# The experts' raw weight chunks in eight rooms, the second unit's list completed on TensorE, the late rows stored from ScalarE's queue

## The chip, the cores and the metric

The kernel runs on one core of one Trainium2 chip. The time is that of one execution on the device, in microseconds; a kernel's time is the median of several executions. Beside it stands one profiled execution, whose trace gives every instruction and DMA; times in the trace count from the start of its span.

## What is computed

The reference is a chain of three layers on 1792 tokens of 768 features:

```
scores = scale * q @ k.T, causal;  x = softmax(scores) @ v        # 4 x 12 heads, 448 x 64
h = x @ w_in;  g = h - tanh(h);  x = g @ w_out                    # 768 -> 2048 -> 768
e_idx = argmax(x @ w_gate)                                        # 8 experts, one for each token
gate_w = softmax(x @ w_gate)[e_idx];  eom = sigmoid(x @ w_output_gate)
out[mask] = gate_w * eom[e] * (relu(x[mask] @ w1[e]) @ w2[e])     # 768 -> 1024 -> 768
```

All data is float32, and which expert a token goes to is known only when its row of the second layer's output is.

## The kernel before

**Precision.** In the large matmuls a float32 operand is split in two parts, a rounded high part (ScalarE, `copy` to float32r) and the rest (VectorE, raw minus high), and three products are summed in PSUM: high by high, high by rest, rest by high. So each weight chunk of 128 x 768 costs a ScalarE cast (line 79) and a subtraction (line 80) before TensorE can use it. The split chunks lie in a ring of slots (class `Weights`, lines 51 to 86), which is filled round and round; a slot is free when the last matmul on its chunk is done.

**Stages.** Attention and the first dense matmul (`attention_mlp1`) run to about 444 us. Then `mlp2_route` makes the second dense layer tile by tile: 14 tiles of 128 tokens, each in two halves of 384 features (`mlp2`, matmuls on line 604), 48 matmuls a half. A tile's rows are stored to the scratch tensor `x2s` in DRAM (line 872, SP's queue). The routing of earlier tiles runs beside it: for the first eleven tiles VectorE multiplies the rows with the eight gate rows, which lie spread over all partitions in `rowsE` (24 KB a partition, lines 564 to 567; the products on line 627); for the last three tiles, and so for the *late* ones, 12 and 13, TensorE turns the rows (`turn`, line 642) and makes the logits (`logits`, line 655). `choose` takes the best expert of each token, `place` counts its position in the expert's list, and `send` (line 761) scatters token number and weight into the list tensor `lst` in DRAM from GpSimd's queue, one scatter for each tile, the second after the first has landed.

**The experts' units.** `experts` works in nine units of up to 256 tokens with one expert's weights, 16 chunks each: eight chunks of w1 (`up`, line 957, 18 matmuls of 256 columns for each chunk) and eight of w2 (`down`, line 977, four calls of 24 matmuls of 384 columns: two token halves `t` by two feature halves `o`). A unit's rows are gathered from `x2s` by an indirect DMA on GpSimd (`gather`, line 908) and turned and split (`split`, lines 945 to 948: twelve transposes in three groups, two PSUM buffers). The results are scattered to the output (`put`, line 989).

The first unit starts early: when tiles 0 to 11 are routed, `begin_with` (lines 775 to 798) picks the fullest expert so far, and its first 256 tokens become the first unit, which needs none of the late tiles. The late tiles' tokens of that expert are placed behind its 256th position (`skip`). The other eight units are the experts 0 to 7 in order, and all their lists are read together, after the late tiles have been sent: `get_lists` (line 825, from GpSimd's queue), then `pick_lists` (line 829: two transposes on line 899, products, `allids` and `allcf` on lines 840 and 841).

**The order of the work.** The Tile framework keeps an order for each engine near that of the program and lets an instruction pass others that are not ready in its own model. Steps of the routing hang in a list `steps` with a due time, counted in quarters of a half-tile (`boundary`, line 845). What is still due when the second layer ends is handed to `experts` as `late`: two steps after each `up` of the first unit (line 1020), the last one, `pick_lists`, in `leave` after the first `down` (line 1027). `leave` also closes the routing's PSUM pool and opens another in its place, so that a `down` behind it can't begin before `pick_lists` has read its PSUM tile; then it gathers the second unit's rows.

**The weights' way.** Raw chunks pass through four stage buffers. The 16 chunks of the first unit are all loaded in the last half of the second layer, one after each of its 16 steps (line 612, `fetch`), each `load` being an SP DMA into a stage buffer, a cast on ScalarE and a subtraction, five of them on GpSimd (`LO_GPSIMD`) and the others on VectorE. Then each `up` is followed by one load and each `down` by two (lines 1018 and 1031). `leave` adds six slots to the ring's 16.

```
 612             after()
1019                 W.append(load(jobs.pop(0)))
1026                 down(hs, W2, y, cu[:, c0 + t:c0 + t + 1], t, o)
1027                 if u == 0 and (t, o) == (0, 0):
1028                     leave()
1029                 if (t, o) == ((1, 0) if u == 0 else (0, 0)) and nxt:
1030                     x = split(xg)
```

## Time and profile before

| | us |
|---|---|
| median of three executions (lowest, highest) | 1043.81 (1043.26, 1045.07) |
| profiled execution, its own time | 1041.34 |
| span of its trace | 1039.7 |
| TensorE busy in it | 995.6 |
| VectorE, ScalarE, GpSimd busy | 656.9, 496.2, 82.0 |

The profiled execution took 1.6 us more than its span, and 2.5 us less than the median of the three others. "PE" is TensorE's matmuls and "PEld" its weight loads, DVE is VectorE, ACT ScalarE, POOL GpSimd, SP SyncE. Durations of matmuls overlap, so that a row of many matmuls is read by its start and by the start of the next row.

### The profile page before, as it was taken

The numbers are of one execution on the slowest core, as the hardware profiler recorded it, in microseconds if no ns is written. First come the engines' busy times: TensorE is split into PE (matmuls) and PEld (weight loads), VectorE is DVE, ScalarE is ACT, GpSimd is POOL, SyncE is SP. The second block draws the span as 40 slices with busy tenths as digits, with TensorE's granted clock in tenths as the row PEclk, the third lists the DMA queues.
The fourth block names the chain that finished last, engine by engine and source line by source line (L and its number), as shares of the span: only waits on it lengthen the run. The fifth ranks groups of instructions, "written<-read, shape, count | busy, mean of one in ns | idle before, by whom it ended". The sixth has DMA issues, their size and how long they took to land.

```text
span 1039.7 us, 16458 instructions
## 1 busy us (share of the span) xinstructions
PE 995.6 (96%) x6068; PEld 891.3 (86%) x6068; DVE 656.9 (63%) x1461; ACT 496.2 (48%) x1027; POOL 82.0 (8%) x87
## 2 busy tenths in 40 slices
PE   8998999999999999999999999986999999999995
PEld 3555788888878888999999999976899999999994
DVE  5888898878787635435767686265556555754520
ACT  5878786677666534311212121253545544654420
POOL 1000000000000000000111112132210111010000
PEclk9999999999999999999999999998999999999998
DMA  8534567566675328452424334376967756764500
GB/s 300 157 131 133 159 176 226 180 213 209 188 212 182 114 92 255 147 217 72 128 88 140 108 91 137 115 240 158 311 190 249 225 191 214 252 205 154 186 14 32
DMA packets 88203, 176.48 MB, mean 170 GB/s; under 512 B 8694, under 2 KB 51944, under 8 KB 87858
## 3 DMA queue, kind: packets, MB, share of 16 engines
q1 hardware_dynamic: 83682, 158.15, 49.0%
q0 software_dynamic: 4272, 16.96, 5.0%
q8 instruction: 49, 0.80, 0.3%
q14 instruction: 40, 0.33, 0.1%
q10 hardware_dynamic: 160, 0.23, 0.1%
HBM read 142.80 MB, written 34.08 MB: 170 GB/s over the span
## 4 chain that ended last, share of the span: by engine, by line
PE 70%; DMA 11%; DVE 8%; ACT 5%; issue 4%; POOL 1%; SPq 1%; POOLq 0%; ACTq 0%; DVEq 0%
PE x2p L604 21%; PE h L414 14%; PE py L977 12%; PE h L957 10%; DMA wraw<-in_w_dram 5%; PE x L391 3%; DMA wo<-dy 3%; PE pt L371 3%; PE s L306 2%; PE s L315 2%; ACT w L79 2%; DMA glo<-gT 1%; DVE w L80 1%; PE warm L436 1%; DVE pr L332 1%
## 5 line engine op out<-in xcount | busy, mean ns | idle before, releaser
L604 PE MATMUL x2p<-w,ghi 128*128 128x384 f32 x896 | 228.7, 336 | 0.0
L414 PE MATMUL h<-xh,w 128*128 128x448 f32 x768 | 225.7, 372 | 1.6 <-DVE g L421 1.0
L80 DVE TENSOR_TENSOR w<-wraw,w 128x768 fp32r<-128x768 f32 x139 | 131.4, 961 | 62.9 <-ACT w L79 61.7
L977 PE MATMUL py<-w,h 128*128 128x384 f32 x864 | 158.2, 340 | 3.9 <-ACT h L963 3.1
L79 ACT CAST w<-wraw 128x768 fp32r<-128x768 f32 x144 | 117.4, 833 | 92.9 <-DMA wraw<-in_w_dram 56.4
L957 PE MATMUL h<-xh,w 128*128 128x256 f32 x864 | 157.9, 285 | 3.9 <-DVE h L964 2.1
L604 PEld LDWEIGHTS x2p<-w,ghi 128*128 128x128 f32 x896 | 161.1, 188 | 0.2 <-issue 0.2
L977 PEld LDWEIGHTS py<-w,h 128*128 128x128 f32 x864 | 150.4, 190 | 4.8 <-ACT h L963 3.4
L604 PE MATMUL x2p<-w,glo 128*128 128x384 f32 x448 | 149.8, 334 | 0.0
L414 PEld LDWEIGHTS h<-xh,w 128*128 128x128 f32 x768 | 138.5, 188 | 11.9 <-DVE g L421 2.2
L414 PE MATMUL h<-xl,w 128*128 128x448 f32 x384 | 141.4, 369 | 0.0
L957 PEld LDWEIGHTS h<-xh,w 128*128 128x128 f32 x864 | 135.2, 192 | 6.3 <-DVE h L964 3.4
L957 PE MATMUL h<-xl,w 128*128 128x256 f32 x432 | 123.1, 285 | 0.1
L341 ACT ACTIVATE pr<-pr,mx 128x128 f32<-128x128 f32 (+3 forms) x168 | 88.8, 529 | 54.8 <-DVE mx L332 53.8
L627 DVE CUSTOM_DVE_ANT_0 junk<-x,rowsE 128x768 bf16<-128x768 f32 x88 | 84.2, 957 | 33.8 <-ACT x L613 31.5
L604 PEld LDWEIGHTS x2p<-w,glo 128*128 128x128 f32 x448 | 84.1, 188 | 0.2 <-issue 0.2
L957 PEld LDWEIGHTS h<-xl,w 128*128 128x128 f32 x432 | 83.2, 193 | 0.3 <-DVE xl L948 0.3
L332 DVE CUSTOM_DVE_ANT_0 pr<-s,mask 128x384 f32<-128x384 f32 (+2 forms) x144 | 59.9, 420 | 29.1 <-PE s L306 21.4
L414 PEld LDWEIGHTS h<-xl,w 128*128 128x128 f32 x384 | 72.0, 188 | 4.3 <-DVE xl L403 0.2
L371 PE MATMUL pt<-ident,pr 128*128 128x128 f32 x384 | 61.8, 276 | 1.3 <-ACT pT L378 0.4
L421 DVE TENSOR_TENSOR g<-h,g 128x448 f32<-128x448 f32 x64 | 39.8, 621 | 34.1 <-ACT g L420 34.0
L391 PE MATMUL x<-pT,v 128*64 128x448 f32 (+3 forms) x384 | 58.0, 399 | 0.3 <-ACT pT L378 0.3
(156 smaller groups left out, 1160.0 us busy)
## 6 DMA issues: line engine op xcount, KB each, us to landing
wraw<-in_w_dram SPq DMA_DIRECT2D x144, 384.0 KB, 3.9
gT<-g SPq DMA_DIRECT2D x64, 224.0 KB, 2.5
glo<-gT SPq DMA_DIRECT2D x14, 1024.0 KB, 5.9
draw<-in_w_out_dram SPq DMA_DIRECT2D x16, 768.0 KB, 4.8
raw<-in_w_in_dram SPq DMA_DIRECT2D x14, 768.0 KB, 5.3
q<-in_qk_dram SPq DMA_DIRECT2D x36, 240.0 KB, 4.1
k<-in_qk_dram SPq DMA_DIRECT2D x36, 224.0 KB, 3.7
wo<-dy SPq DMA_DIRECT2D x16, 384.0 KB, 5.3
```

The source lines that it names most:

```text
L79: self.nc.scalar.copy(t[:, 0, :], raw)
L80: lo_engine.tensor_tensor(t[:, 1, :], raw, t[:, 0, :].bitcast(F32), op=ALU.subtract)
L332: nc.vector.tensor_tensor_reduce(out=self.probs(r), in0=ss[:, o:o + w], in1=m, scale=-0.125, scalar=3.0e38, op0=ALU.add, op1=ALU.min, accu ...
L341: nc.scalar.activation(pc, pc, AF.Exp, bias=self.mx[:, x:x + 1], scale=-1.0, accum_out=self.sm[:, x:x + 1],)
L371: nc.tensor.transpose(pt[:, n * P:(n + 1) * P], self.pr[:, o:o + P], ident)
L391: nc.tensor.matmul(px[j * D:(j + 1) * D, kc * P:], self.v[:n, kc, j, :], self.pT[:n, j, pcol[kc]:pcol[kc] + S - kc * P], start=(kc == 0), ...
L414: nc.tensor.matmul(ph, w[:, kd, :], x, start=(n == 0), stop=(n == 3 * KD - 1))
L421: nc.vector.tensor_tensor(g, ph, g, op=ALU.subtract)
L604: nc.tensor.matmul(px, a[:, f, :], w[:, 0, h * hn:(h + 1) * hn], start=(n == 0), stop=(n == 3 * NF - 1),)
L627: nc.vector.tensor_tensor_reduce(out=junk, in0=x2, in1=row, scale=1.0, scalar=0.0, op0=ALU.mult, op1=ALU.add, accum_out=to,)
L957: nc.tensor.matmul(ph, wp[:, kd, :], a[:, kd].rearrange("p a b -> p (a b)"), start=(n == 0), stop=(n == 3 * KD - 1),)
L977: nc.tensor.matmul(py, hs[f][a][:, c], w[:, 0, o * hn:(o + 1) * hn], start=(n == 0), stop=(n == 3 * KF - 1),)
```

## The change

- `Supply` holds eight *rooms* of 128 x 768. At first they hold the eight gate rows (one DMA each in place of two for four rows each); when `begin_with` is through, the first unit's and all experts' chunks are entered, and `fill` issues DMAs into rooms as they come free. `load` splits the next raw chunk and calls `fill`. Only the first eight chunks are split in the last half of the second layer (after its steps 0 to 7), the other eight after the first unit's `up`s. All subtractions are VectorE's. The ring grows by two slots and not by six, and two more chunks are loaded after the first unit.
- The second unit is now expert 0 from a list of its own, `early`: `get_early` reads that expert's list as the first twelve tiles left it, `pick_early` turns it, and `add_late` adds the late tiles' tokens with one-hot matmuls on TensorE; then it gathers the rows. The list of the other seven is read as before, but `leave` comes after the third `down` of the first unit.
- The late steps go one, one, two, two, one after the first five `up`s (`LATER`), `turn` before them.
- The rows of tiles 12 and 13 are stored from ScalarE's queue and not from SP's.

```diff
+LATER = (1, 1, 2, 2, 1, 0, 0, 0)
-LO_GPSIMD = (3, 4, 7, 13, 15)
...
-    def split(self, raw, a, lo_engine):
+    def split(self, raw, a):
         t = self.slot()
         self.nc.scalar.copy(t[:, 0, :], raw)
-        lo_engine.tensor_tensor(t[:, 1, :], raw, t[:, 0, :].bitcast(F32), op=ALU.subtract)
+        self.nc.vector.tensor_tensor(t[:, 1, :], raw, t[:, 0, :].bitcast(F32), op=ALU.subtract)
-    def load(self, stage, src, a, lo_engine):
-        raw = stage.tile([P, 768], F32, tag="wraw", name="wraw")
-        self.nc.sync.dma_start(raw, src)
-        return self.split(raw, a, lo_engine)
...
+class Supply:
+    def __init__(self, nc, ring, pool, nrooms):
+        self.nc, self.ring, self.pool, self.n = nc, ring, pool, nrooms
+        self.pos = 0
+        self.todo, self.raws, self.W = [], [], []
+    def room(self, i, name):
+        return self.pool.tile([P, 768], F32, tag=f"room{i}", name=name, bufs=1)
+    def add(self, chunks):
+        self.todo.extend(chunks)
+    def fill(self):
+        while self.todo and len(self.raws) < self.n:
+            src, a = self.todo.pop(0)
+            raw = self.room(self.pos, "wraw")
+            self.nc.sync.dma_start(raw, src)
+            self.raws.append((raw, a))
+            self.pos = (self.pos + 1) % self.n
+    def load(self):
+        if self.raws:
+            self.W.append(self.ring.split(*self.raws.pop(0)))
+            self.fill()
+    def take(self, n):
+        W = self.W[:n]
+        del self.W[:n]
+        return W
...
-    rowsE = dotp.tile([P, E, DM], F32, name="rowsE")
-    for h in range(2):
-        s = slice(h * E // 2, (h + 1) * E // 2)
-        nc.sync.dma_start(rowsE[:, s], gates[s].unsqueeze(0).to_broadcast([P, E // 2, DM]))
+    rowsE = [supply.room(e, f"row{e}") for e in range(E)]
+    for e in range(E):
+        nc.sync.dma_start(rowsE[e], gates[e:e + 1].to_broadcast([P, DM]))
...
+        one = w12[bass.ds(first[0], 1)].rearrange("e f p c -> (e f) p c")
+        supply.add(weight_chunks(one, KD, w12.shape[1] // 2))
+        for e in range(E):
+            supply.add(weight_chunks(w12[e], KD, w12.shape[1] // 2))
+        supply.fill()
...
+    def get_early():
+        src = lst.rearrange("(r b) c -> r (b c)", b=P)[0:4, :]
+        early.append(fetch_list(nc, sp, src, 4))
+    def pick_early():
+        pt = turn_list(nc, ps, early[0], 4, ident)
+        both = sp.tile([P, 2, 2, 2], F32, tag="both0", name="both0", bufs=1)
+        for r in range(2):
+            nc.vector.tensor_scalar_mul(
+                both[:, r], pt[:, :, 2 * r:2 * r + 2], is1[:, r, 0:1]
+            )
+        had = sp.tile([P, 2, 2], F32, tag="had", name="had", bufs=1)
+        nc.vector.tensor_tensor(had, both[:, 0], both[:, 1], op=ALU.add)
+        start = sp.tile([P, 1], F32, tag="start", name="start", bufs=1)
+        nc.vector.tensor_scalar(
+            start, is1[:, 1, 0:1], -2.0 * P, 1.0, op0=ALU.mult, op1=ALU.add
+        )
+        early.extend([had, start])
+    def add_late(route):
+        _, had, start = early
+        N = route.n
+        v = sp.tile([P, 2], F32, tag="v", name="v", bufs=1)
+        nc.vector.scalar_tensor_tensor(
+            v, route.po, start, route.oh[:, :, 0], op0=ALU.add, op1=ALU.mult
+        )
+        to = sp.tile([P, 2, 2 * P], F32, tag="to", name="to", bufs=1)
+        add = sp.tile([P, 2, 2], F32, tag="add", name="add", bufs=1)
+        nc.vector.tensor_scalar_add(add[:, :, 0], tok[:, LATE:LATE + N], -float(NT))
+        nc.vector.tensor_copy(add[:, :, 1], route.pr[:, :, 1])
+        for m in range(N):
+            nc.vector.tensor_scalar(
+                to[:, m], slots, v[:, m:m + 1], None, op0=ALU.is_equal
+            )
+        pq = ps.tile([P, 2, 2], F32, tag="tr", name="late")
+        for t in range(2):
+            for m in range(N):
+                nc.tensor.matmul(
+                    pq[:, t, :], to[:, m, t * P:(t + 1) * P], add[:, m, :],
+                    start=(m == 0), stop=(m == N - 1),
+                )
+        for n, nm in enumerate(("ids", "cf")):
+            nc.vector.tensor_tensor(
+                consts["early" + nm], pq[:, :, n], had[:, n, :], op=ALU.add
+            )
+        early.append(gather(nc, consts["xg"], x2s, consts["earlyids"], 0))
...
-                mlp2(t, g, x2, h, (lambda: fetch(first[0])) if last else None)
+                mlp2(t, g, x2, h, (lambda f: f < NF // 2 and supply.load()) if last else None)
...
-            nc.sync.dma_start(x2s[t * P:(t + 1) * P, :], x2)
+            put = nc.scalar if t >= LATE else nc.sync
+            put.dma_start(x2s[t * P:(t + 1) * P, :], x2)
...
         if t0 + N == LATE:
-            then += [(6, begin_with), (11, begin_x)]
+            then += [(6, begin_with), (7, get_early), (11, begin_x), (12, pick_early)]
         if t0 + N == NTT:
+            then[-1:-1] = [(p, lambda r=route: add_late(r))]
             then += [(9, totals), (9, get_lists), (13, pick_lists)]
...
-    jobs = [job for e in range(E) for job in weight_chunks(w12[e], KD, KF)]
-    todo = [(consts["ids"], consts["cf"], 0)]
-    todo += [(consts["allids"], consts["allcf"], 2 * e) for e in range(E)]
+    todo = [(consts[nm + "ids"], consts[nm + "cf"], 0) for nm in ("", "early")]
+    todo += [(consts["allids"], consts["allcf"], 2 * e) for e in range(1, E)]
     x = split(xg)
+    late.pop(0)()
     def leave():
-        nonlocal ps, xg
+        nonlocal ps
         while late:
             late.pop(0)()
         route_close()
         rp = ctx.enter_context(tc.tile_pool(name="ring2", bufs=1))
-        ring.add_slots(rp, 6)
+        ring.add_slots(rp, 2)
         ps = ctx.enter_context(tc.tile_pool(name="exps", bufs=2, space=PSUM))
-        xg = gather(nc, consts["xg"], x2s, todo[1][0], todo[1][2])
     for u, (iu, cu, c0) in enumerate(todo):
-        W1, W2, W = W[:KF], W[KF:2 * KF], W[2 * KF:]
         nxt = todo[u + 1] if u + 1 < len(todo) else None
         if u > 0 and nxt:
             xg = gather(nc, consts["xg"], x2s, nxt[0], nxt[2])
         hs = []
+        W1 = supply.take(KF)
         for f in range(KF):
             hs.append(up(x, W1[f], f))
-            if jobs:
-                W.append(load(jobs.pop(0)))
-            for _ in range(2):
-                if len(late) > 1:
+            supply.load()
+            if u == 0:
+                for _ in range(LATER[f]):
                     late.pop(0)()
+        if u == 0:
+            xg = early[-1]
+        W2 = supply.take(KF)
         for t in range(2):
             y = sp.tile([P, DM], F32, tag="y", name="y")
             for o in range(2):
                 down(hs, W2, y, cu[:, c0 + t:c0 + t + 1], t, o)
-                if u == 0 and (t, o) == (0, 0):
-                    leave()
                 if (t, o) == ((1, 0) if u == 0 else (0, 0)) and nxt:
                     x = split(xg)
                 for _ in range(2):
-                    if jobs:
-                        W.append(load(jobs.pop(0)))
+                    supply.load()
+                if u == 0 and (t, o) == (1, 0):
+                    leave()
             put(y, iu[:, c0 + t:c0 + t + 1])
+        if u == 0:
+            for _ in range(2):
+                supply.load()
...
-        consts["stage"] = ctx.enter_context(tc.tile_pool(name="stage2", bufs=4, side="right"))
+        rooms = ctx.enter_context(tc.tile_pool(name="rooms", bufs=1, side="right"))
+        consts["supply"] = Supply(nc, ring, rooms, E)
```

## Rows read from the trace of the kernel before

**Rows 1.** The page's second part: TensorE's busy tenths in 40 slices of the span.

```profile
PE   8998999999999999999999999986999999999995
```

**Rows 2.** Busy time by stage: stretch, us, then each engine, granted clock, DMA share, GB/s.

```profile
682.46:741.98 59.52, 45.29 (x293) 41.30 (x292) 34.68 (x70) 27.98 (x49) 18.18 (x14) 0.89 0.75 217
741.98:780.03 38.05, 36.19 (x254) 35.31 (x253) 22.95 (x32) 19.71 (x32) 4.05 (x4) 1.00 0.71 226
780.03:815.99 35.96, 35.68 (x254) 35.21 (x253) 20.71 (x30) 18.09 (x29) 3.95 (x4) 1.00 0.67 216
816.15:851.37 35.22, 35.22 (x255) 34.95 (x254) 20.76 (x30) 17.99 (x29) 3.95 (x4) 1.00 0.67 215
725.00:730.00 5.00, 4.43 (x18) 4.46 (x19) 3.98 (x10) 3.03 (x4) 3.56 (x3) 0.66 0.44 117
```

**Rows 3.** The chain that ended last, fourth unit: start us, us, what.

```profile
816.15 17.11 PE h L957 x144
833.27 4.17 PE py L977 x24
837.43 0.87 PE tr L945 x8
```

**Rows 4.** TensorE in order of time around the first unit; idle time before in brackets.

```profile
682.46 1.03 PE L945 MATMUL tr<-ident,xg 128*128 128x128 f32 x8
...
685.63 0.98 PE L957 MATMUL h<-xh,w 128*128 128x256 f32 x6 [1.58 <-ACT xh L947]
...
693.42 0.63 PE L655 MATMUL lg<-x2T,gw 128*32 128x256 f32 x6 [2.21 <-ACT x2T L645]
...
695.67 0.87 PE L671 MATMUL g<-fold,lgT 128*128 128x16 f32 x4
...
717.86 0.80 PE L977 MATMUL py<-w,h 128*128 128x384 f32 x2 [3.05 <-ACT h L963]
...
724.52 0.44 PE L899 MATMUL ltr<-ident,li 32*128 32x32 f32 x2 [4.93 <-DMA li<-lst]
725.57 9.87 PE L977 MATMUL py<-w,h 128*128 128x384 f32 x48 [0.60 <-DVE allids L840]
```

**Rows 5.** GpSimd's timeline in the same stretch.

```profile
659.31 0.96 POOL L761 DMA_INDIRECT lst<-pr,sl  x1 [9.82 <-DVE sl L754]
663.86 0.59 POOL L892 DMA_DIRECT2D li<-lst  x1 [3.59 <-DMA lst<-pr,sl]
672.14 1.05 POOL L908 DMA_INDIRECT xg<-x2s,ids  x1 [7.69 <-DVE cf L804]
...
704.92 1.54 POOL L761 DMA_INDIRECT lst<-pr,sl  x1 [1.60 <-DVE ov L822]
713.62 0.98 POOL L761 DMA_INDIRECT lst<-pr,sl  x1 [7.16 <-DMA lst<-pr,sl]
719.47 0.64 POOL L892 DMA_DIRECT2D li<-lst  x1 [4.87 <-DMA lst<-pr,sl]
```

**Rows 6.** ScalarE's timeline: a DMA issue at the start, and the first unit.

```profile
1.54 0.87 ACTq L264 DMA_DIRECT2D k<-in_qk_dram  x1
...
683.21 0.47 ACT L613 COPY x<-x2p 128x384 f32<-128x384 f32 x1
...
713.60 0.83 ACT L79 CAST w<-wraw 128x768 fp32r<-128x768 f32 x1 [3.53 <-DMA wraw<-in_w_dram]
```

**Rows 7.** Instructions on the experts' raw chunks: ns min/median/max, first and last start.

```profile
L80 DVE TENSOR_TENSOR w<-wraw,w x139: 936/959/1732, 675.4 to 991.1; 128x768 fp32r<-128x768 f32 x139
...
L80 POOL TENSOR_TENSOR w<-wraw,w x5: 1837/1935/2475, 677.6 to 701.4; 128x768 fp32r<-128x768 f32 x5
```

**Rows 8.** DMA issues between 662 and 668 us, KB each, us to landing.

```profile
x2s<-x SPq DMA_DIRECT2D x1, 384.0 KB, 4.4
```

**Rows 9.** DMA landings on the tensor of the second layer's rows.

```profile
DMA to landing us min/median/max: 2.7/5.1/10.5
```

**Rows 10.** DMA landings of the gathers, line 908.

```profile
DMA to landing us min/median/max: 3.8/4.6/10.5
```

More of the change, by code (lines that the diff above doesn't have):

```diff
@@ L535, in split_w @@
     def split_w(f):
-        wout.append(ring.split(raws.pop(0), 1, nc.vector))
+        wout.append(ring.split(raws.pop(0), 1))
         fetch_w(f + 4)
@@ L590, in mlp2_route @@
     )
+    slots = cp.tile([P, 2 * P], F32, name="slots")
+    nc.gpsimd.iota(
+        slots, pattern=[[1, 2 * P]], base=1, channel_multiplier=0,
+        allow_small_or_imprecise_dtypes=True,
+    )
     ones = cp.tile([P, P], BF16, name="ones")
@@ L841, in pick_lists @@
         nc.vector.tensor_tensor(consts["allcf"], both[:, 0, 1], both[:, 1, 1], op=ALU.add)
-    steps, first = [], []
+    steps, first, early = [], [], []
     def boundary(now):
@@ L886, in mlp2_route @@
     consts["rtps"] = ps
-    return first[2], [st for _, st in sorted(steps, key=lambda x: x[0])], ctx.close
+    late = [st for _, st in sorted(steps, key=lambda x: x[0])]
+    return first[2], early, late, ctx.close
 def fetch_list(nc, pool, src, n):
@@ L919, in weight_chunks, with experts @@
         yield e[f], KD if f < KF else 1
-def experts(tc, consts, ring, load, W, xg, late, route_close, w12, x2s, lst, out):
+def experts(tc, consts, ring, xg, early, late, route_close, w12, x2s, lst, out):
     nc = tc.nc
@@ L1081, in fused @@
     consts = dict(ident=ident, S=S, D=D, NP=NP, B=NT // S)
-    for nm, n in (("", 2), ("all", 2 * E)):
+    for nm, n in (("", 2), ("early", 2), ("all", 2 * E)):
         consts[nm + "ids"] = cp.tile([P, n], I32, name=nm + "ids")
@@ L1105, in fused @@
     last = attention_mlp1(tc, consts, ring, qk, v, w_in, w_out, wo, gT)
-    def load(job):
-        n = consts["nload"] = consts.get("nload", -1) + 1
-        return ring.load(consts["stage"], *job, nc.gpsimd if n in LO_GPSIMD else nc.vector)
-    W, first = [], []
-    def fetch(e):
-        if not first:
-            one = w12[bass.ds(e, 1)].rearrange("e f p c -> (e f) p c")
-            first.extend(weight_chunks(one, DM // P, KF))
-        W.append(load(first[len(W)]))
-    xg, late, close = mlp2_route(tc, consts, ring, last, wo, gw, gates, gT, x2s, lst, fetch)
-    experts(tc, consts, ring, load, W, xg, late, close, w12, x2s, lst, out)
+    xg, early, late, close = mlp2_route(
+        tc, consts, ring, last, wo, gw, gates, w12, gT, x2s, lst
+    )
+    experts(tc, consts, ring, xg, early, late, close, w12, x2s, lst, out)
 def laid_out(np, q, k, v, moe_w_in, moe_w_out, moe2_w_gate, moe2_w_output_gate, moe2_w1, moe2_w2):
```

25 lines of the change are left out of this document (16 added, 9 removed).

## The prediction

> **What bounds the kernel now.** The slices come first [rows 1]: TensorE is at 9 tenths nearly throughout, with one dip behind slice 26, some 680 to 760 us. Nothing outside it is worth much to this change, which touches neither attention nor the first dense layer. The stages size the dip [rows 2]: the first unit, from the end of the second layer to the first `up` of the next, takes 59.52 us, the second 38.05, the third 35.96, the fourth 35.22 with TensorE busy all the time. The fourth's pace is the matmuls themselves [rows 3]: 144 `up`s in 17.11, four `down`s of 4.17, twelve transposes in some 1.4. Three units at that pace would be 105.7; they take 133.5. So about 28 us are lost, and not all can come back: the first unit also holds its own transposes and the routing of the late tiles.
>
> TensorE's order of time says who holds it [rows 4]. The first `up` begins 3.2 us after the first transpose. Later come 2.21 us for `x2T` on ScalarE, 3.05 for a relu on ScalarE, and 4.93 for the list of all experts, with 1.05 more from its transposes to the next `down`. Behind the first two of these stands a late weight: ScalarE's casts wait for their DMAs, as at 713.60 [rows 6], and relus and copies queue behind them. After the long wait the granted clock is 0.66 of full, between its levels of 1.2 and 2.4 GHz [rows 2], and 48 matmuls take 9.87 us [rows 4] where two `down`s take 8.3 [rows 3]: 1.5 us on top. The list's 4.93 has a chain of its own on GpSimd [rows 5]: first scatter at 704.92, second only when it has landed, at 713.62, the list's read at 719.47, landed at 724.5.
>
> **The change part by part.** *Rooms.* Eight raw chunks are asked for at about 662 us, 12 us before the last half of the second layer, and afterwards eight are always on their way in place of four. At 4.4 us to land [rows 8] the first eight are there before their casts begin; the waits for weights go. Casts and subtractions remain. The five subtractions of GpSimd, 1.9 us each, become five of VectorE, 0.96 each [rows 7]: 4.8 us, costed at nothing, because VectorE was busy 34.7 of the first unit's 59.5 us [rows 2], and even all of that with these 4.8 and an estimated 1.5 for the late list's small operations is 41 of the 43 us that I expect of the unit. It is near: where subtractions bunch, VectorE is what is late next, at 0.96 a chunk. The gate rows' eight DMAs in place of two move the same bytes, hidden by the first tile's half-layers; costed at nothing.
>
> *Late rows from ScalarE.* An issue on ScalarE takes 0.87 us in the nearest row [rows 6], against the wait and the cast that now stand between its copy at 683.21 and the first `up` at 685.63. Two issues, one of them on the path: I let them cancel most of the gain and take 685.0 as the first `up` (bounds 684 and 686.5). SP is then free for the loads; the store shares the DMA engines with them.
>
> *The second unit's list.* `add_late` adds four float32 matmuls of two columns. The nearest row has two matmuls of 16 columns, four records, in 0.87 us at a lowered clock [rows 4]; so 1.7 at most, nothing if they fall into waits, and I take 0.9. The two small transposes of `pick_early` and the VectorE operations lie beside the second layer. On GpSimd two gathers, 1.05 us of issue each [rows 5], now stand before the scatters of the late tiles, and `out`'s scatters behind all of it.
>
> *The first unit, summed.* First `up` 685.0; `up`s 17.1; routing left on TensorE 2.0 (an estimate from the 0.63 and 0.87 of [rows 4] and the turn) and the new 0.9; three `down`s 12.5; transposes for the second unit 1.4. These can't hide under the fourth `down`, which stands behind `leave`: between 0 and the 3.2 us that the same chain left uncovered at 682.46; I take 1.1, since no store stands in it. That is 720.0. Then the list's transposes and `allids`, 1.05 as before: 721.05.
>
> *The list's wait* is what is late next. The scatter comes after four `up`s in the program, 696 at the earliest; before it came at 704.92, which with two gathers makes 707.0 at the latest; I take 701, as the chain from `x2T` to `sl` loses 2.2 us of waiting and its VectorE operations the company of GpSimd's. From first scatter to landed list before took 19.6 [rows 4, 5]; with both scatters at the 4.55 from 659.31 to 663.86 and the read's 5.0 it is 14.1. So the list lands at 715 to 720.6, and I put no wait; the bounds are 0 and 707.0 + 19.6 + 1.05 - 721.05 = 6.6 us. The fourth `down` then ends at 725.2, against 741.98: 16.8 us less.
>
> *Second and third unit* come to the fourth's 35.22: 2.8 and 0.7 less. The ring of 18 slots is enough in the program's order: a chunk goes to the slot of the one 18 before it, whose matmuls are over by then. The last unit's end and the output's scatter stay.
>
> The sum is 20.3 us, so the profiled execution's 1041.3 becomes 1021.0. It ran 2.5 us below the median of the three runs; on their scale the time is 1043.8 - 20.3 = **1023.5 us**.
>
> **The rivals.** *The list still holds TensorE.* For it: the read, both scatters and the pool switch are as before, with gathers ahead. If the first scatter goes at 704.9 and the chain takes 19.6, `allids` is at 725.6, 4.5 us late, and a wait of that kind cost 1.5 us of clock: 1029.5. Against it: the waits that delayed the scatter go.
>
> *The first gather is late.* It reads `x2s`, and so waits for tile 12's store, now beside eight loads instead of four. On SP that store took 4.4 us [rows 8], and the gathers began at 672.14, after the list and not after the store [rows 5]. If it takes the longest landing of its kind, 10.5 [rows 9], it ends at 676.2; second gather at 677.3, landed by at most 10.5 more [rows 10] at 687.8, where TensorE began on it at 682.46: 5.3 us, with the clock 6.8, so 1030.3. A rule speaks for this rival: the Trainium skill, page "DMA: Bandwidth & Descriptors", section "Issuing engines are not separate DMA queues", says that all queues run on the same DMA engines and interleave, so that another queue saves issue time only. By that rule the store meets the eight loads all the same; the sum above takes no gain for the queue either.
>
> *The weights come no earlier where it counts.* A room is refilled only after VectorE's subtraction; if the middle of the first unit still waits its 3.05 us and loses clock, 4.6 us of the gain go: 1028.
>
> *Slower.* Two slots more in place of six leave two split chunks in hand and not six. If casts run later than that, every unit waits for weights in its `up`s as the second one does now, at 38.05. Seven units then lose 2.1 + 6 x 2.83 = 19.1 us, against 16.8 from the first: 1046.1. It decides from 37.8 us a unit on. Against it: ScalarE and VectorE are busy 18 and 21 us of 35.2 in the fourth unit [rows 2], and DMAs are asked for eight chunks ahead.
>
> **How the numbers follow.** The forecast has 0.68, with a range of its own of 1019 to 1028 (start, added matmuls and transposes at their bounds, and the list's round trip hidden or a few us late). The list has 0.13, the gather 0.07, the weights 0.05, the slower unit 0.06, no change that can be told 0.01. A difference of 0.2%, 2.1 us, is about what can be told from no change here. So faster 0.93, same 0.01, slower 0.06. The range of 8 in 10 takes in the first two rivals for the most part: 1018 to 1031.
>
> **What would show it.** Right: the first unit at some 43 us, no wait on TensorE for a relu behind a cast, the second unit at 35 to 36; the early gathers issued before 700 and landed long before the second unit's transposes; the list's read landing at about the third `down`'s end. Wrong in parts: an idle stretch before line 899's successor (the list), a wait of the first unit's transposes on the gather, a granted clock below 1 in either. Wrong altogether: units beyond the third longer than 35.5 us, with their `up`s or `down`s waiting for a cast or subtraction.

## The result, and the profile after

The changed kernel takes 1030.89 us (median, 1028.55 to 1034.49) beside 1044.42 for the kernel before on the same chip: a ratio of 0.9875, with a 95% interval from 0.9837 to 0.9912. On the 1043.8 us of the forecast that is 13.0 us less, with an interval of 9.2 to 17.0; the forecast was 20.3 less. The profiled execution took 1028.57 us. Three lines of its page, the first with busy time, share of the span and instructions, the others the 40 slices of TensorE and of its granted clock:

```profile
PE 996.1 (97%) x6078; PEld 892.4 (87%) x6078; DVE 659.5 (64%) x1477; ACT 491.8 (48%) x1027; POOL 77.4 (8%) x84
...
PE   8998999999999999999999999999999999999995
...
PEclk9999999999999999999999999999999999999998
```

The dip behind slice 26 [rows 1] is gone at this scale. By stage, with the columns of [rows 2]: the first two units together (from the first transposes to the third unit's first `up`), the third and the fourth.

```profile
685.71:768.24 82.53, 78.20 (x553) 75.89 (x552) 51.15 (x104) 41.48 (x74) 16.07 (x14) 0.98 0.71 243
768.24:803.63 35.39, 35.39 (x253) 35.12 (x252) 20.92 (x30) 17.41 (x30) 4.60 (x4) 1.00 0.66 218
803.63:839.08 35.45, 35.45 (x253) 35.18 (x253) 20.93 (x30) 17.45 (x30) 4.58 (x4) 1.00 0.64 216
```

The first two units took 97.57 us before [rows 2] and take 82.53. (They are told together because some of the second unit's `up`s now run ahead of the first unit's last `down`.) From the third on TensorE is busy all the time. What it still waits for between 680 and 800 us, as line, releaser, us in total, times, longest:

```profile
PE h L1054 <- DVE h L1061: 2.2, 1, 2.2
PE h L1054 <- ACT xh L1044: 2.1, 2, 1.9
```

The waits of [rows 4] for `x2T`, for the list and for a relu in the first unit are gone, and two are there in their place.

**Runs are compared by the stretch** from the start of the first unit's transposes to the end of the span: 1027.0 - 685.71 = 341.3 us here, 1039.7 - 682.46 = 357.3 before (from the unrounded spans). What lies ahead of it scatters from one execution to the next: in two executions of the kernel before, the second dense layer begins at 443.9 and 448.1 us, in three of the changed one at 446.6, 450.0 and 445.9. From there to the first transposes it is steadier: 238.6 and 238.3 us before, 239.1, 238.9 and 239.0 after, so some 0.5 us more. The forecast of 20.3 us less means a stretch of 337.0.

**The first wait** is before the first `up`. ScalarE in order of time, idle time before and its releaser in brackets:

```profile
677.71 5.99 ACT L79 CAST w<-wraw 128x768 fp32r<-128x768 f32 x8 [0.57 <-PE x2p L639]
683.92 0.84 ACT L79 CAST w<-wraw 128x768 fp32r<-128x768 f32 x1 [0.23 <-PE x2p L639]
685.00 0.84 ACT L79 CAST w<-wraw 128x768 fp32r<-128x768 f32 x1 [0.24 <-DMA wraw<-in_w_dram]
686.72 0.83 ACT L79 CAST w<-wraw 128x768 fp32r<-128x768 f32 x1 [0.87 <-DMA wraw<-in_w_dram]
687.46 0.47 ACT L648 COPY x<-x2p 128x384 f32<-128x384 f32 x1
...
688.56 1.07 ACT L1044 CAST xh<-tr 128x512 fp32r<-128x512 f32 x2
```

The first eight chunks had landed, as forecast. But the framework, which orders each engine's instructions, has put the casts of chunks nine to eleven ahead of the second layer's last copy, though in the code they stand behind the first `up`s. Those chunks are refills of rooms just freed; for the tenth and the eleventh ScalarE waits on their DMAs, and copy and `xh` casts wait behind. TensorE pays twice here, in idle time and in clock, as its timeline and three stretches of 2 us show:

```profile
685.71 1.03 PE L1042 MATMUL tr<-ident,xg 128*128 128x128 f32 x8
...
689.20 1.22 PE L1054 MATMUL h<-xh,w 128*128 128x256 f32 x5 [1.89 <-ACT xh L1044]
```

```profile
687.00:689.00 2.00, 0.31 (x6) 0.00 (x0) 1.99 (x3) 2.00 (x4) 0.00 (x0) 1.00 1.01 393
689.00:691.00 2.00, 1.80 (x9) 1.80 (x10) 2.00 (x4) 2.00 (x5) 0.00 (x0) 0.62 1.01 312
691.00:693.00 2.00, 2.00 (x12) 2.00 (x11) 2.00 (x3) 1.73 (x5) 0.00 (x0) 0.53 1.01 393
```

The first `up` starts 3.49 us after the first transposes, not 2.5, and then runs until about 693 us at a granted clock near half, the lower of its two levels (1.2 and 2.4 GHz). The first `down` starts 25.7 us after the transposes; the forecast's terms make 22.5.

**The second wait** grows earlier than it is paid. DMA share and GB/s are the last two columns:

```profile
716.00:726.00 10.00, 9.76 (x61) 9.42 (x60) 1.86 (x4) 1.66 (x3) 1.70 (x2) 1.00 0.29 102
726.00:736.00 10.00, 10.00 (x73) 9.83 (x73) 8.36 (x17) 7.75 (x12) 5.87 (x5) 1.00 0.53 153
736.00:746.00 10.00, 7.80 (x65) 7.60 (x64) 4.72 (x8) 5.25 (x9) 0.76 (x1) 1.00 1.01 393
```

With the casts run ahead, the ring's 16 slots are full by 716 us: 24 chunks are cast, the last at 711.9, into 16 slots of which the first eight `up`s have freed eight. The next cast needs a slot that only `leave` adds, and waits for `allcf`, the last result of the steps that `leave` runs. ScalarE is busy 1.66 of 10 us; no room comes free, no load is issued between 716 and 726, and the DMA engines are busy for 0.29 of the time. After `leave` everything comes at once:

```profile
728.43 4.51 ACT L79 CAST w<-wraw 128x768 fp32r<-128x768 f32 x6 [1.26 <-DVE allcf L933]
...
737.38 2.30 ACT L79 CAST w<-wraw 128x768 fp32r<-128x768 f32 x3 [1.79 <-DMA wraw<-in_w_dram]
...
741.05 0.83 ACT L79 CAST w<-wraw 128x768 fp32r<-128x768 f32 x1 [1.08 <-DMA wraw<-in_w_dram]
744.17 0.83 ACT L79 CAST w<-wraw 128x768 fp32r<-128x768 f32 x1 [2.29 <-DMA wraw<-in_w_dram]
744.90 0.38 ACT L1060 ACTIVATE h<-h 128x256 fp32r<-128x256 f32 x1
```

Six casts free six rooms; the eleven loads issued from 728 to 746 us land after a median 8.2 us, beside four gathers (7.4 us) and a scatter of `out`. The relu at 744.90 stands behind a cast that waited 2.29 us, VectorE's part of the same `h` (line 1061) behind the relu, and TensorE's next `up` behind both. Load, KB and us to landing, then TensorE:

```profile
wraw<-in_w_dram SPq DMA_DIRECT2D x11, 384.0 KB, 8.2
```

```profile
745.79 0.51 PE L1054 MATMUL h<-xh,w 128*128 128x256 f32 x2 [2.20 <-DVE h L1061]
```

That ScalarE is a strict first-in-first-out queue is also said by the Trainium skill, page "TensorE: Matmul & The Clock Gate", section "Architectural detail: the array is 16× 32×32, not 1× 128×128"; ScalarE's lines above agree: nothing passes a waiting cast.

GpSimd's lines, to compare with [rows 5]:

```profile
675.59 1.03 POOL L1004 DMA_INDIRECT xg<-x2s,ids  x1 [7.86 <-DMA x2s<-x]
...
704.48 0.99 POOL L796 DMA_INDIRECT lst<-pr,sl  x1 [26.58 <-DVE units L905]
706.54 1.58 POOL L1004 DMA_INDIRECT xg<-x2s,earlyids  x1 [1.07 <-DVE tot L913]
...
718.13 0.64 POOL L988 DMA_DIRECT2D li<-lst  x1 [5.74 <-DMA lst<-pr,sl]
```

The first gather does wait for tile 12's store, but its rows are there in time. The early gathers go at 706.54, not before 700, and still land long before they are needed. TensorE does not wait for the list, nor for these rows.

### The profile page after: what moved, and what is told of

Its sections match the earlier page's. It is cut to its first block, busy times and chain, and to the rows that moved or that the text cites. A ratio compares the mean times of both kernels' runs of the same rounds, so it can differ in the third digit from the quotient of the medians.

```text
span 1027.0 us, 16510 instructions
## 1 busy us (share of the span) xinstructions
PE 996.1 (97%) x6078; PEld 892.4 (87%) x6078; DVE 659.5 (64%) x1477; ACT 491.8 (48%) x1027; POOL 77.4 (8%) x84
## 4 chain that ended last, share of the span: by engine, by line
PE 81%; DVE 6%; DMA 5%; ACT 4%; issue 2%; SPq 0%; POOL 0%; POOLq 0%; ACTq 0%; DVEq 0%
PE x2p L639 22%; PE h L443 16%; PE h L1054 14%; PE py L1074 14%; PE x L420 4%; PE pt L400 3%; PE s L335 3%; DMA wo<-dy 2%; PE s L344 2%; DMA wraw<-in_w_dram 2%; PE warm L465 1%; PE tr L1042 1%; DVE pr L361 1%; DMA glo<-gT 1%; DVE dy L151 1%
## 5 line engine op out<-in xcount | busy, mean ns | idle before, releaser
L1074 PE MATMUL py<-w,h 128*128 128x384 f32 x864 | 155.3, 336 | 0.0
L79 ACT CAST w<-wraw 128x768 fp32r<-128x768 f32 x144 | 113.9, 830 | 36.8 <-PE py L1074 28.5
L662 DVE CUSTOM_DVE_ANT_0 junk<-x,row 128x768 bf16<-128x768 f32 x88 | 84.2, 957 | 33.1 <-ACT x L648 30.8
L400 PEld LDWEIGHTS pt<-ident,pr 128*128 128x128 f32 x384 | 46.1, 140 | 14.2 <-ACT pT L407 1.8
```

Of the source, the lines that this page charges most:

```text
L79: self.nc.scalar.copy(t[:, 0, :], raw)
L400: nc.tensor.transpose(pt[:, n * P:(n + 1) * P], self.pr[:, o:o + P], ident)
L662: nc.vector.tensor_tensor_reduce(out=junk, in0=x2, in1=row, scale=1.0, scalar=0.0, op0=ALU.mult, op1=ALU.add, accum_out=to,)
L1074: nc.tensor.matmul(py, hs[f][a][:, c], w[:, 0, o * hn:(o + 1) * hn], start=(n == 0), stop=(n == 3 * KF - 1),)
```

## The experiments

All are edits of the changed kernel but two of the kernel before. "Stretch" is as above; the column after it tells when the third unit's first `up` starts, from the first transposes. Both come from the one profiled execution of a row, and the ratio from executions of the kernel before on the same chip.

| run | median us (range) | ratio to before, 95% | stretch | third unit |
|---|---|---|---|---|
| before, first profile | 1044.42 (1043.26–1045.07) | | 357.3 | 97.6 |
| b_again | 1042.93 (one) | | 354.9 | 96.9 |
| changed, first profile | 1030.89 (1028.55–1034.49) | 0.9875 [0.9837, 0.9912] | 341.3 | 82.5 |
| a_again | 1031.31 (1024.53–1034.05) | 0.9897 [0.9857, 0.9937] | 343.4 | 84.9 |
| a_third | 1029.59 (1026.61–1032.31) | 0.9887 [0.9852, 0.9922] | 343.5 | 84.6 |
| v_pin | 1033.51 (1029.04–1036.59) | 0.9934 [0.9905, 0.9963] | 346.3 | 87.3 |
| v_pinall | 1023.96 (1023.23–1026.60) | 0.9843 [0.9809, 0.9877] | 335.5 | 76.9 |
| v_pinall2 | 1024.46 (1023.78–1027.87) | 0.9838 [0.9813, 0.9863] | 335.5 | 76.9 |
| v_gather | 1025.71 (one) | | 338.8 | 80.1 |
| v_pinall_g | 1029.03 (1027.39–1033.83) | 0.9888 [0.9839, 0.9938] | 341.7 | 82.8 |
| v_oldlist | 1031.29 (1027.04–1032.16) | 0.9912 [0.9882, 0.9942] | 343.2 | 84.6 |
| v_old_pin | 1032.45 (1030.28–1033.55) | 0.9905 [0.9870, 0.9940] | 344.6 | 86.0 |
| v_listpin | 1027.64 (1027.12–1030.26) | 0.9879 [0.9850, 0.9907] | 341.3 | 82.7 |
| v_n4 | 1037.02 (1033.83–1039.64) | 0.9958 [0.9939, 0.9977] | 346.9 | 87.8 |
| v_pinall_n4 | 1029.72 (1025.73–1032.24) | 0.9888 [0.9840, 0.9935] | 340.2 | 81.4 |
| v_sp | 1032.23 (1029.35–1034.04) | 0.9918 [0.9891, 0.9946] | 345.7 | 86.9 |
| v_pinall_sp | 1027.47 (1023.09–1028.86) | 0.9856 [0.9821, 0.9892] | 336.7 | 77.8 |
| b_pin | 1037.64 (1035.37–1040.33) | 0.9953 [0.9933, 0.9973] | 350.8 | 92.6 |

**Both kernels again** (a_again, b_again, a_third): no edit.

> The changed kernel once more, as the reference for the runs beside it. What is open: the part before the second dense layer, which the change does not touch, took 2.8 us longer in its trace than in the trace of before (first matmul of the second layer at 446.6 against 443.9 us). If that comes from the program (addresses, order), it is there again, 2 to 3 us; if it is scatter from execution to execution, this trace and the repeated one of before differ by less than 1 us or the other way round. Time: 1028 to 1034 us.

> The kernel before once more, for its trace on the same chip. By program: first matmul of the second layer at 443 to 444.5 us; by scatter: anywhere from 443 to 447. Time 1041 to 1045 us.

> The changed kernel once more, on the chip of the runs beside it: 341 to 344 us from the first transposes to the end, time 1028 to 1032.

The changed kernel's stretch is 341.3 to 343.5, that of before 354.9 to 357.3: 13.4 us between the means (342.7 and 356.1). With the 0.5 us that the second layer lost, that agrees with the ratio's 13.0. Of the forecast stretch of 337.0, 4 to 6 us are missed.

The two waits are there in all three traces of the changed kernel: 1.9, 1.6 and 1.7 us at their longest for the `xh` casts, 2.2, 2.6 and 3.0 us for the relu. What they cost in clock differs. After the first wait the clock falls in the first profile and in a_again, and stays at 1.00 in a_third; after the second it stays at 1.00 in the first profile, and falls to 0.50 for 2 us in a_again and to 0.53 and 0.61 in a_third.

**The casts of the first unit's eight W2 chunks held in program order** (v_pin).

```diff
...
-        self.nc.scalar.copy(t[:, 0, :], raw)
+        cast = self.nc.scalar.copy(t[:, 0, :], raw)
+        if keep:
+            keep(cast)
...
-            supply.load()
+            supply.load(tc.keep_in_program_order if u == 0 else None)
```

> The changed kernel with ScalarE's casts of the first unit's eight second-layer chunks held in program order, behind the relu of the up they follow. My theory: three of these casts stand ahead of the last copy of the second layer's rows on ScalarE and wait there for their DMAs, which delays the first unit's transposed rows by 1 to 1.5 us and, through the idle TensorE, lowers the clock over its first ups (some 2 us more). Then the first up starts 2.0 to 2.7 us after the first transpose in place of 3.5, the granted clock stays at 1.0, and the kernel is 2.5 to 4 us faster than the changed one. Rival: the wait is the chain of transposes, casts and subtraction itself; then the first up moves by under 0.5 us, the clock still falls, and the time is the same within 1 us.

Counted from the first transposes, the first `up` starts at 1.72 us and the first `down` at 22.4, 3.3 us sooner than in the changed kernel's first profile. But the kernel is no faster (stretch 346.3 beside 341.3 to 343.5): casts that aren't held now pass those that are. The cast at 710.48 is not held; a relu of the first unit stands behind it, and behind the relu the last held cast, at 712.48, for which TensorE's first `down` waits. ScalarE's timeline and TensorE's waits:

```profile
710.48 0.83 ACT L79 CAST w<-wraw 128x768 fp32r<-128x768 f32 x1 [4.65 <-DMA wraw<-in_w_dram]
...
712.20 0.38 ACT L1062 ACTIVATE h<-h 128x256 fp32r<-128x256 f32 x1
```

```profile
PE h L1056 <- DVE h L1063: 3.3, 1, 3.3
PE py L1076 <- ACT w L79: 2.9, 1, 2.9
```

The start was diagnosed rightly, and the loss moved on to the next cast that was free to run ahead.

**Cast and subtraction of every chunk that the units load held** (v_pinall, v_pinall2), behind `up`s and `down`s alike; only the first eight chunks, split in the second layer, are not.

```diff
-        self.nc.scalar.copy(t[:, 0, :], raw)
-        self.nc.vector.tensor_tensor(t[:, 1, :], raw, t[:, 0, :].bitcast(F32), op=ALU.subtract)
+        keep(self.nc.scalar.copy(t[:, 0, :], raw))
+        keep(self.nc.vector.tensor_tensor(t[:, 1, :], raw, t[:, 0, :].bitcast(F32), op=ALU.subtract))
...
-            supply.load()
+            supply.load(keep)
```

> The changed kernel with the cast and the subtraction of every chunk that the experts load held in program order on ScalarE and VectorE, not only those of the first unit's ups. My theory, as the last runs leave it: what the change loses is lost where a cast that is not needed yet stands ahead of a relu or a copy in ScalarE's queue and waits for its DMA, at the first unit's start and again in the second unit's ups; holding eight casts only moved the place. Then the first up comes 1.5 to 2 us after the first transpose, no TensorE wait over 1 us is left behind a relu, a cast or a subtraction in the first two units, the third unit starts 77 to 80 us after the first transpose (82.5 and 84.9 in the two traces of the changed kernel, 87.3 with eight held), and the stretch from the first transpose to the end is 335 to 339 us against 341 and 343. Rival: the weights' DMAs themselves are the limit there (393 GB/s, no idle DMA engine in 736 to 746); then the waits only move to the matmuls that use the chunks, and the third unit starts at 82 us or later.

> A repeat of the changed kernel with the casts and subtractions of the experts' chunks held in program order, beside the changed kernel on the same chip. Theory A (the order of the casts is what was lost): 335 to 337 us from the first transposes to the end, no wait of TensorE over 0.5 us in the first two units, time 5 to 8 us below the changed kernel's. Rival B (the first run was a lucky one): 338 to 342 us and at most 3 us below.

The stretch is 335.5 us both times, and the median of v_pinall2 lies 5.1 us below a_third's on its chip (1029.59 - 1024.46). The executions' ranges overlap between 1026.6 and 1027.9 us; the stretch tells the two kernels apart. Of v_pinall2, ScalarE before the first `up`, TensorE's only wait of 0.2 us or more between 665 and 800 us, and the first two units and the third:

```profile
682.80 5.99 ACT L79 CAST w<-wraw 128x768 fp32r<-128x768 f32 x8 [0.57 <-DMA wraw<-in_w_dram]
691.00 0.48 ACT L648 COPY x<-x2p 128x384 f32<-128x384 f32 x1 [2.21 <-PE x2p L639]
```

```profile
PE h L1054 <- ACT xh L1044: 0.2, 1, 0.2
```

```profile
690.80:767.70 76.90, 76.55 (x552) 74.29 (x551) 48.08 (x99) 37.63 (x68) 15.55 (x14) 1.00 0.77 242
767.70:803.20 35.50, 35.50 (x255) 35.23 (x254) 21.33 (x29) 17.53 (x29) 4.75 (x4) 1.00 0.65 214
```

After the first eight, ScalarE waits 2.21 us for TensorE and not for a DMA, the copy goes 0.20 us after the first transposes (1.75 in the changed kernel), and the clock stays full. The gap in the transfers closes too; in v_pinall, whose first transposes stand at 687.31:

```profile
716.00:726.00 10.00, 9.76 (x63) 9.25 (x62) 4.80 (x10) 4.27 (x7) 1.70 (x2) 1.00 0.72 221
726.00:736.00 10.00, 10.00 (x74) 9.96 (x73) 5.74 (x11) 5.74 (x11) 5.86 (x5) 1.00 0.68 217
736.00:746.00 10.00, 9.94 (x84) 9.70 (x83) 8.48 (x15) 6.15 (x12) 0.04 (x1) 1.00 0.98 355
```

DMA share 0.72 where it was 0.29; the same late burst (0.98) delays nobody. So neither DMA bandwidth nor the number of slots was the limit, but the order of the casts with their subtractions (the two were not held apart).

**The gathers from the third unit on held in program order** on GpSimd, in the changed kernel (v_gather) and in the one with the casts held (v_pinall_g).

```diff
-        nc.gpsimd.indirect_dma_start(
+        keep(nc.gpsimd.indirect_dma_start(
...
-            xg = gather(nc, consts["xg"], x2s, nxt[0], nxt[2])
+            xg = gather(nc, consts["xg"], x2s, nxt[0], nxt[2], tc.keep_in_program_order)
```

> The changed kernel with the gathers of the third unit on held in program order on GpSimd, so that the four gathers of 0.4 MB each that come together in the second unit are spread over two units. If the burst of gathers on top of the refilled rooms makes the casts wait (DMA as the limit), the second unit loses 2 to 4 us less and the third starts at 79 to 81 us after the first transpose. If it is the order of the casts alone, the third unit starts at 82 to 85 as before.

> The changed kernel with the cast and the subtraction of every expert chunk held in program order, and also the gathers from the third unit on held in program order on GpSimd. Theory A (the burst of refills and gathers hurts only because casts stand ahead of urgent work in ScalarE's queue): with the order held, the gathers cost nothing, and from the first transposes to the end it takes 335 to 336.5 us, as with the casts held alone (335.5); time 1023 to 1025 us. Rival B (the burst is a cost of its own, on the transfers): another 1.5 to 3 us come off, 332.5 to 334 us, time 1020.5 to 1022.5.

In the changed kernel the stretch is 2.5 to 4.7 us shorter, in one execution, and the second wait does not appear: two of the four gathers of the burst start at 735.39 us and not at 728.91, the other two after 768, and the casts go on sooner, the twelfth behind `leave` at 737.93 us and not at 741.05. With the casts held it turns round, against both readings of the text above. The gathers for the third unit now start 46.0 us after the first transposes (41.6 in v_pinall):

```profile
736.15 0.69 PE L1042 MATMUL tr<-ident,xg 128*128 128x128 f32 x2 [3.39 <-DMA xg<-x2s,allids]
```

```profile
736.00:746.00 10.00, 9.85 (x61) 9.85 (x62) 3.12 (x5) 2.55 (x6) 0.00 (x0) 0.70 0.70 251
```

TensorE reaches the third unit's first transposes before their rows, and runs the next 10 us at a granted clock of 0.70. The stretch is 6.2 us longer than without. Where casts were late, holding the gathers seems to have helped (one trace); with the casts held it did harm.

**The second unit's list as before** (v_oldlist, v_old_pin, v_listpin): the whole list read after the last scatter, pools released behind the first `down`; rooms, loads and store stay changed.

```diff
-            then[-1:-1] = [(p, lambda r=route: add_late(r))]
...
+                if u == 0 and (t, o) == (0, 0):
+                    leave()
```

> The changed kernel with the old list: the second unit is again read from the list of all experts, leave after the first down. Rooms, the store from ScalarE and the ring stay. By the sum: the waits for weights are gone, the wait for the list is there; the list lands at some 17 to 20 us after the first scatter, so that TensorE waits 6 to 12 us at its transposes, with a lowered clock after it. I expect the third unit at 89 to 95 us after the first transpose, and 1033 to 1040 us; so the list is worth 7 to 12 us of the 15. Rival: the rooms bring nearly all, the list little: third unit at 82 to 86.

> Casts and subtractions of the experts' chunks held in program order, and the list of the second unit built as before (whole list read after the last scatter, pools released behind the first down); rooms, depth and store as in the changed kernel. Theory A (the early list is worth what the forecast gave it, but in the changed kernel the late casts hid that): the second unit waits for its list and gathers again, and from the first transposes to the end it takes 340 to 343 us against 335.5 with the early list; time 1028 to 1031. Rival B (the list is worth little here, since the work of the second unit can be put ahead of the wait): 335.5 to 337.5 us, time 1023.5 to 1026.

> The changed kernel with the casts and subtractions held in program order and with the list of the second unit built as before (whole list read after the last scatter, pools released behind the first down). Theory A (the early list is worth what the forecast gave it, but the late casts of the changed kernel hid that): TensorE waits 3 us or more for the list or for the second unit's rows, and it takes 340 to 343 us from the first transposes to the end against 335.5 with the early list. Rival B (the list is worth little here, since the second unit's work can stand ahead of the wait): 335.5 to 337.5 us, time within 2 us of the run with the early list.

The kernel that ran as v_old_pin did not hold the order of its casts; it is a second run of v_oldlist, and v_listpin is the run that its text describes. In the changed kernel the old list gives 343.2 and 344.6, beside 341.3 to 343.5 with the early one: worth little, and no more than the three traces with the early list differ among themselves. Once the order is held it is 341.3 against 335.5 (medians 1027.64 and 1024.46). In v_listpin TensorE's waits are

```profile
PE ltr L994 <- DMA li<-lst: 4.7, 1, 4.7
PE py L1073 <- DVE allids L932: 0.6, 1, 0.6
```

5.3 of the 5.8 us. The early list takes that wait away, as forecast. In the changed kernel the second wait, for the relu, comes in its place. With the old list the casts stop for `leave` too (DMA share 0.32 from 706 to 716 us in v_oldlist), but after the first `down`, and TensorE then waits for no relu; with the early list `leave` comes after the third `down`, and the wait follows. That the place of `leave` makes this difference is not isolated by a run.

**Four chunks on their way in place of eight** (v_n4, and with the order held v_pinall_n4).

```diff
-        consts["supply"] = Supply(nc, ring, rooms, E)
+        consts["supply"] = Supply(nc, ring, rooms, E // 2)
```

> The changed kernel with four chunks on their way in place of eight (the gate rows keep eight rooms). If the depth is what takes the waits for weights away, the first unit waits again 3 us or more for casts behind their DMAs, and the third unit starts 3 to 8 us later than in the changed kernel. If depth is not needed, since only the place of the casts in ScalarE's queue counts, it is within 2 us.

> Casts and subtractions held in program order as above, but four raw chunks on their way in place of eight. Theory A (eight rooms bring transfers early enough, depth is a cost of its own): 338 to 341 us from the first transposes to the end against 335.5, time 1026.5 to 1029. Rival B (the order of the casts is all, four are deep enough once it is held): 335 to 336.5 us, time 1023 to 1025.

The depth is worth 3.4 to 5.6 us without the order and 4.7 with it. In v_pinall_n4 TensorE waits for ScalarE's `xh` and VectorE's `h` again:

```profile
PE h L1054 <- ACT xh L1044: 2.0, 2, 1.7
PE h L1054 <- DVE h L1061: 1.1, 1, 1.1
```

**The late rows stored from SP as before** (v_sp, v_pinall_sp).

```diff
-            put = nc.scalar if t >= LATE else nc.sync
-            put.dma_start(x2s[t * P:(t + 1) * P, :], x2)
+            nc.sync.dma_start(x2s[t * P:(t + 1) * P, :], x2)
```

> The changed kernel with tiles 12 and 13 stored from SP's queue as before. My theory: the queue makes little difference to the transfers, but on SP the store of tile 12 stands behind loads that wait for a room, and tile 13's behind those that wait for subtractions; the first gather then waits longer for tile 12's store. I expect the first gather's issue 0 to 3 us later than with ScalarE's queue, still before it is needed, and the early gathers not delayed; time the same within 2 us. Rival: on ScalarE the issue delays the first up (0.3 to 0.9 us each), so that the kernel is 0.5 to 1.5 us faster with SP. Second rival: SP's order makes the store of tile 12 so late that TensorE waits for the first unit's rows, 5 us or more slower.

> The order held as in the run beside it, and the late rows stored from SP as before. Theory A (the store's queue costs nothing, as forecast): 335 to 337 us and the same time within 2 us. Rival B (from SP the store of the row tile that the first gather needs stands behind eight loads of chunks, as in the run with the stores from SP alone, where TensorE waited 1.3 us for the gathered rows): TensorE waits 1 to 3 us for the first gathered rows, which lie ahead of the first transposes, so the span up to them grows, not what follows; time 1 to 3 us longer.

The stretch is 2.2 to 4.4 us longer in the changed kernel, though the medians on one chip, 1032.23 and 1031.31, don't tell the two apart; it is 1.2 longer with the order held, where the executions' ranges overlap (1023.09 to 1028.86 beside 1023.78 to 1027.87). On SP the store of tile 12 stands behind eight loads, whose issue takes 4.40 us in v_pinall_sp:

```profile
669.70 4.40 SPq L103 DMA_DIRECT2D wraw<-in_w_dram  x8
674.21 0.37 SPq L965 DMA_DIRECT2D x2s<-x  x1
```

The first gather then goes 7.56 us ahead of the first transposes (682.61 and 690.17) and not 9.79 (681.01 and 690.80 in v_pinall2). The store is issued 15.96 us ahead of them and not 17.73. In v_sp TensorE waited 1.3 us for the gathered rows; in v_pinall_sp its weight loads for the first transposes waited 0.41 us for them, and the first `down` starts 0.9 us later (23.25 us after the first transposes, 22.35 in v_pinall2). What makes the rest of the 1.2 us is open.

**The kernel before with its casts and subtractions held** (b_pin), the same `keep` in its units.

> The kernel before, with nothing changed but that the cast and the subtraction of each chunk that the experts load keep their program order on their engines. Theory A (in the kernel before, too, it is the order of the casts on ScalarE that holds the units up, and rooms are not needed): at most 348 us from the first transposes to the end against 355 to 357, time 7 or more below the kernel before. Rival B (before, a load is issued only when one of four staging tiles is free, and that late issue is the cost): 353 to 358 us, the time within 3 us of the kernel before; were the casts in program order later than where they stood, it could be up to 5 us slower.

The order alone is worth 4.9 us there (0.47% of 1042.68; interval 2.8 to 7.0), with a stretch of 350.8 between the two readings of the text above. What is left is seen in its ScalarE and TensorE's waits:

```profile
685.41 0.83 ACT L79 CAST w<-wraw 128x768 fp32r<-128x768 f32 x1 [1.43 <-DMA wraw<-in_w_dram]
686.15 0.58 ACT L947 CAST xh<-tr 128x512 fp32r<-128x512 f32 x1
```

```profile
PE ltr L899 <- DMA li<-lst: 6.1, 1, 6.1
PE h L957 <- ACT xh L947: 2.3, 1, 2.3
```

The cast at 685.41 stands where the code has it, ahead of the `xh` casts (it is the first unit's eighth), and still waits for a load, of which only four are on their way; the list's wait is the longest of all. Rooms, early list and order are each needed for the whole gain.

## Why the prediction was right in sign and wrong in size

The sum is that of a kernel whose casts keep their order: a stretch of 337.0 us was forecast, 335.5 is measured there, 341.3 to 343.5 in the changed kernel, whose casts don't keep it. Of the 7.3 us that the times fall short (20.3 less 13.0), 5.7 are this difference at the mean of three traces, 0.5 the second layer's, and 1.2 come from the first profile of the kernel before, which was the longer of its two.

On the forecast's scale the measured time is 1030.8 us (1043.8 x 0.9875). That lies outside the 1019 to 1028 of the forecast itself and just inside the range of 1018 to 1031, at the edge that was left for the list and the gather, neither of which was late. That the wide range held is luck. Point by point:

- *"The waits for weights go"* is the step that failed, and *"take 685.0 as the first `up`"* with it. I costed the casts in the program's order, and that order is what the changed kernel does not keep. Eight chunks landed early; the ninth to eleventh were cast ahead of the second layer's last copy and waited for their DMAs. The term of 2.5 us to the first `up` is 3.2 to 3.5 (1.71 with the order held, in v_pinall), and up to the first `down` it is 25.2 to 25.8 where my terms give 22.5 and the held order 22.4: some 3 us. In the first profile about half of that is clock; in a_third none is.
- *"The ring of 18 slots is enough in the program's order"* was true as worded and did not apply. Run ahead, the casts filled 16 slots before `leave` added two, and the loads stopped. I took "eight are always on their way" for granted and weighed the two slots only for the late units. Together with the first wait this makes the first two units 82.5 to 84.9 us, where 42.7 + 35.2 = 77.9 was forecast and 76.9 is reached with the order held.
- *The list's wait*: none, as I put it. What the early list takes away is there (5.8 us with the order held), but in the changed kernel about 1 us of it arrives (a mean of 343.9 in the two runs with the old list, 342.7 in the three without), less than those runs scatter.
- *Costed at nothing.* VectorE's five added subtractions: rightly, with 51.15 us busy of 82.53. The second layer, with the early list's added work in it, is some 0.5 us longer. The store on ScalarE, which I gave no gain for its queue, is worth 1.2 us or more by the stretch, in one trace on either side. The page I cited there, the Trainium skill's "DMA: Bandwidth & Descriptors", section "Issuing engines are not separate DMA queues", leaves a new queue the issue time alone. The rows agree: SP's issue of eight loads took 4.40 us, the store's issue gained 1.8 and the gather 2.2. I passed over that this time lay ahead of a gather.
- *The rivals.* "The weights come no earlier where it counts" came nearest, in its time (1028) and in that casts still wait; but the place is not the one it named, and the cause is the order, not the subtractions that free a room. The list did not hold TensorE; the gather waited 7.86 us and was in time; the third and the fourth unit take 35.39 and 35.45 us (above) and those behind them 35.3 to 35.5, far from the 37.8 at which the slower rival decides.

What stays open: the 4.9 us of b_pin are not split further, and how much of the burst's harm came from the gathers and how much from the stopped loads is only bounded, by the 2.5 to 4.7 us of v_gather's one trace.

## What to carry to other kernels

Loading further ahead pays in full only if what consumes the loads keeps its place: on an engine that works in order, as ScalarE does in these rows, a cast hoisted in front of urgent work waits for its DMA on behalf of all that stands behind it. Before a staging depth is sized, look in the trace at the order in which the consuming engine really runs, and pin it where the framework may reorder; here that alone was worth 5.8 to 8.0 us of the stretch, and pinning only some of the casts moved the wait and won nothing. Pin no more than that: with the gathers pinned as well, 6.2 us of it were lost again.

## What was not expected of the hardware

- A TensorE idle time of 1.89 us was followed by a granted clock of 0.62 and 0.53 (the rows of 689 to 693 us above). In the same execution an idle time of 2.20 us cost no clock:

```profile
743.00:745.00 2.00, 0.59 (x5) 0.39 (x4) 0.00 (x0) 0.83 (x2) 0.00 (x0) 1.00 1.02 407
745.00:747.00 2.00, 1.21 (x10) 1.21 (x11) 1.69 (x3) 2.00 (x5) 0.00 (x0) 1.00 1.04 412
```

  In a_third it was the other way round: 1.74 us at the first place cost none, 3.00 us at the second was followed by 0.53 and 0.61. And 3.39 us in v_pinall_g was followed by 0.70 over 10 us. The length of a stop alone does not tell its price; this may be part of the 2 us by which the changed kernel's traces differ.
- At a DMA share of 1.01 and 393 GB/s a chunk's load took 8.2 us to land in the median, and one on the chain to the second wait 10.39, against the 4.4 us of one store [rows 8] from which I worked.
- The part that the change doesn't touch begins the second layer anywhere from 443.5 to 451.8 us in these profiles, while v_pinall and v_pinall2, 3.6 us apart there, agree to 0.1 us in the stretch. A change of a few us is read from the stretch and not from the span.
